# A two-layer spectral and MLP-mixer kernel: stores on GpSimd's queue, u split over two products, an earlier scale, and one weight load moved ahead

## The chip, the cores and the metric

The kernel runs on one core of a Trainium2 chip. The metric is the device time of one execution in microseconds (us), the median of several runs. Engines are called as in the profile: PE (TensorE), DVE (VectorE), ACT (ScalarE), POOL (GpSimd), SP (SyncE, which here only issues DMAs).

## The reference

Two kinds of layer alternate, twice, on x of 2048 tokens by 640 channels. The change lies in the second kind, B.

```python
def _A_ref(x, w_r, w_i):                       # spectral filter
    X = jnp.fft.rfft2(x, axes=(-2, -1)) * (w_r + 1j * w_i)
    return jnp.fft.irfft2(X, s=(S, D), axes=(-2, -1))

def _B_ref(x, w1, b1, w2, b2):                 # MLP over the tokens
    h = _layernorm(x, axis=-1)                 # (B, 2048, 640)
    u = jnp.einsum("bsd,sf->bdf", h, w1) + b1  # (B, 640, 1728)
    u = _gelu(u)                               # tanh form
    y = jnp.einsum("bdf,fs->bds", u, w2) + b2  # (B, 640, 2048)
    return y.transpose(0, 2, 1)

x = x + _A_ref(_layernorm(x), A_w_r, A_w_i)
x = x + _B_ref(_layernorm(x), B_w1, B_b1, B_w2, B_b2)
x = x + _A_ref(_layernorm(x), A_w_r, A_w_i)
x = x + _B_ref(_layernorm(x), B_w1, B_b1, B_w2, B_b2)
```

## The kernel before, in words

`run()` goes through the two layers. In each the spectral filter comes first and the MLP behind it; the MLP of layer 1 is `b1st`, that of the last layer `b2nd`. All large products run on PE in float16 with each operand split in two halves, high and low: a product is the sum high x high + low x high + high x low. The splits of weights cost ACT one pass (high half, `wh`) and DVE one (low half, `wl`), and so it is with the activations: DVE makes `uh` and `ul` from the gelu's output `uf` (`usplit`).

**`b1st`.** The first product runs over 14 tiles of w1 (`ft` counts them; `SEQ` gives the order in which tiles come: 6, 13, 0, 7, 1, 8, 2, 9, 3, 10, 4, 11, 5, 12, so that a pair of tiles with even and odd `ft` is d and d+7). Each of these is 96 matmuls, 16 steps `j` of 6. Raw weights in float32 are loaded by `wload` on SP's queue, in two parts into two buffers; ACT sums their squares (`scan1`, output `junk`), and a short chain of DVE and PE steps (`scale1`: a DVE reduction into `sqb`, PE's product with `ones`, a few DVE steps on one column) makes the scale by which the tile is split (`wsplit`). The steps of that chain are called by `step(m)` at places that are written into the loops by hand, tile m being one of w1 (m below 14) or of w2 (m = 14 and up).

Since the last layer uses the same w1 and w2, layer 1 stores what it has split: `wstore` stores w1's halves (`w1A..`, 36 stores of 256 KB) and some of w2's, and `wssplit` makes four sums of each pair of w1 tiles (S1 to S4, made by `wsum` in float32) into high and low halves, in one of two buffers `sp`, and stores them (`w1S..`, 24 stores of 512 KB). The last layer uses them for products by Strassen's scheme. All these stores stand on SP's queue, among the raw loads.

The gelu of a tile (ACT: `t`, square `q`, tanh; DVE: `q`, `uf`) follows its product. The scale of u is known from `scale_u`, called at ft = 11, j = 8. The 14 `usplit`s come in the last product (ft = 13, from j = 6 on, tiles 0 to 9) and behind the loop (10, 11, 13, 12). The second product then takes 16 tiles of w2, with all 14 tiles of u for each, in `SEQ`'s order.

**`b2nd`.** The same two products, by Strassen's scheme: `one` is a list of 42 products with w1 (N1 = 42), `two` one of 56 with w2, numbered n from 0. A product of the second list is 21 matmuls; the first four are 18 each at first, and the seventh tile of u (`LATE`) is added for all four at n = 3. The weights go through six buffers in turn (`place`: wo0, wo1, and wl, wh twice). `fetch` loads a stored part into the next buffer on SP's queue; `form`, `hi` and `lo` make a sum of raw parts (DVE `S`), its high half (ACT) and its low half (DVE) instead, from raw w2 loaded by `load2`. `xload` loads rows of x to which the result is added (`xt`). The first six parts of the second list, A11.0 to A22.1, are w2's and were stored by layer 1; these are the quarters spoken of here, A22.1 the sixth. In the loop before, turn n fetches part n + 4, after that turn's product is issued.

Each engine works through its instructions in order. The order on each engine is that of the code where `self.pin` is set, and elsewhere that of a scheduler, which sets instructions by their dependencies and costs; `b1st`'s two products lie outside the pin. Buffers are reused in turn, and a writer waits for the last reader.

Of the kernel before, what the change touches and what calls it, by code (L numbers as in the profile page):

```python
# [20 lines left out]
NJ, NG, NFT = 16, 16, 14  # L21
# [8 lines left out]
SEQ = [t + 7 * i for t in (6, 0, 1, 2, 3, 4, 5) for i in range(2)]  # L30
# [36 lines left out]
class Layers:  # L67
# [813 lines left out]
    def wstore(self, m, w):  # L881

        k, t, n = self.wtile(m)
        e = t % NQ if k else t % 7
        if (not 6 <= e < 8) if k else e == 6:
            return
        for c in (0, 1) if t == e else (1,):
            a, q = f"A{1 + (t > e)}{c + 1}", n // 2
            st = (self.ws2 if k else self.ws1)[e][a]
            for i in range(2):  # L890
                self.nc.sync.dma_start(st[:, i], w[i][:, c * q:c * q + q])

    def wsum(self, m, a):

# [6 lines left out]
    def wssplit(self, m, a):  # L901

        d = SEQ[m - 1]
        s = self.s1p[:, d:d + 1]
        w = self.t(self.pz, [128, 2, 8, 128], F16, "sp", 2)
        self.T.activation(w[:, 0], self.sums[a], AF.Identity, scale=s)
        self.V.scalar_tensor_tensor(w[:, 1], self.sums[a], s, w[:, 0], op0=ALU.mult, op1=ALU.subtract)
        self.nc.sync.dma_start(self.ws1[d][a], w)

    def b1st(self, li):  # L910
        nc, A = self.nc, self.A
# [13 lines left out]
        for j in range(NJ):  # L925
            self.h.append((self.hh[j], ph.tile([128, 2, 320], F16, name=f"hl{j}_{self.n}")))
            V.tensor_tensor(self.h[j][1], self.hf[j], self.hh[j], op=ALU.subtract)
            if j == 11:
                next(sc[2])
        self.pin = False  # L930
        self.pop("hf")
# [5 lines left out]
        uf = [pf.tile([128, 2, 320], F32, name=f"uf{f}_{self.n}") for f in range(NFT)]  # L937
# [23 lines left out]
        def usplit(ft, t):  # L961
            V.tensor_scalar(uh[ft], t, self.su, None, op0=ALU.mult)
            c = slice(0 if ft < NFT - 1 else 64, 128)
            V.scalar_tensor_tensor(ul[ft][c], t[c], self.su[c], uh[ft][c], op0=ALU.mult, op1=ALU.subtract)
            if ft == NFT - 1:
                V.tensor_copy(ul[ft][:64], uh[ft][:64])
                G.memset(uh[ft][64:], 0.0)
# [18 lines left out]
        w = self.w.pop(0), self.w.pop(1)  # L986
        pss = self.big(), self.big()
        self.both_high(pss, w, prod)
        for ft in range(NFT):
            if ft < 2:  # L990
                ps, run = pss[ft], rest(ft, pss[ft], w[ft])
                if ft:
                    self.wopen(2)
            else:
                ps = self.big()
                w2 = self.w.pop(ft)
                run = both(ft, ps, w2)
                ahead(ft, w2)
            steps = prep(ft)
            for j in run:  # L1000
                if ft % 2 and ft < NFT - 2 and 11 <= j < 15:
                    self.wsum(ft + 2, ("S1", "S3", "S2", "S4")[j - 11])
                if ft > 1:
                    m = ft + 1 - ft % 2
                    d = SEQ[m - 1]
                    if ft < m and j == 7:
                        q = [self.st[0][:, t:t + 1] for t in (d, d + 7)]
                        V.tensor_tensor(self.s1p[:, d:d + 1], *q, op=ALU.min)
                    if j in ((9, 14) if ft < m else (1, 7)):
                        self.wssplit(m, {9: "S1", 14: "S2", 1: "S3", 7: "S4"}[j])  # L1010
                if ft == 0:
                    if j in (6, 7):
                        step(2)
                elif ft == 1:
                    if j in (1, 2):
                        next(steps)
                    if j in (8, 10):
                        self.scan1(3, (j // 2 - 4,))
                    if j == 15:
                        step(3)  # L1020
                else:
                    if ft == 2 and j in (4, 5):
                        step(3)
                    if ft == 2 and j in (5, 6):
                        self.scan1(4, (j - 5,))
                    if ft == 2 and j == 7:
                        step(4)
                    if j in ((6, 8) if ft == 2 else (2, 4)):
                        next(steps)
                    if ft == 2 and j in (10, 11) or ft > 2 and j in (4, 5):  # L1030
                        step(ft + 2)
                    if j == 8 and ft == NFT - 3:
                        self.scale_u()
                    if j in (11, 13):
                        self.scan1(ft + 3, (j // 2 - 5,))
                    if j == 15:
                        step(ft + 3)
                    if ft == NFT - 1 and 6 <= j:
                        usplit(j - 6, uf[j - 6])
            dup, i = ft == 1, SEQ[ft]  # L1040
            pv, bb, c1 = ps[:, :, :320], self.b1[:, i:i + 1], self.ct[0][:, i:i + 1]
            if dup:

                sw = self.t(p, [128, 2, 320], F32, "sw", 1)
                T.activation(sw[:64], pv[64:], AF.Copy)
                T.activation(sw[64:], pv[:64], AF.Copy)
                V.tensor_tensor(sw, pv, sw, op=ALU.add)
                pv = sw
            t = self.t(p, [128, 2, 320], F32, "t", 2)
            q = self.t(p, [128, 2, 320], F32, "q", 2)  # L1050
            T.activation(t, pv, AF.Identity, scale=c1, bias=bb)
            T.activation(q, pv, AF.Square, scale=c1, bias=bb)
            V.scalar_tensor_tensor(q, q, 1.0 / GC, t, op0=ALU.add, op1=ALU.mult)
            T.activation(q, q, AF.Tanh, scale=GS * GC)
            V.scalar_tensor_tensor(uf[i], q, 1.0, t, op0=ALU.add, op1=ALU.mult)
        for k in (10, 11, 13, 12):
            usplit(k, uf[k])
        self.pop("uf")
        self.pop("b1")
# [25 lines left out]
        for j in range(NJ):  # L1085
# [14 lines left out]
            if tail:  # L1100

                order.sort(key=lambda q: q[1])
                st = self.t(p, [128, 2, 6], F32, "st", 2)
# [55 lines left out]
    def b2nd(self, li):  # L1159
# [29 lines left out]
        N1, NP = len(one), len(one) + len(two)  # L1189
# [17 lines left out]
        def fetch(n):  # L1207
            if n >= NP or not kept(n):
                return
            d, a, _ = ops[n]  # L1210
            w = place(n, 8 if n < N1 else 7)
            if n < N1:
                nc.sync.dma_start(w, self.ws1[d][a])
            else:
                nc.sync.dma_start(w, self.ws2[E[d]][a])
                if a[2] == "2":
                    G.memset(w[64:, :, 6], 0.0)
# [163 lines left out]
        for d in range(ND):  # L1381
            i = {a: at[d, a] for a in PB}
# [139 lines left out]
        def xload(d):  # L1522
            if d < NQ:
                xts[d] = self.t(p, [128, 2, 2, 320], F32, "xt", 3)
                for i in range(2):
                    nc.sync.dma_start(row(d, i), self.xs[li][E[d] + NQ * i])
# [59 lines left out]
        for (d, a), n in at2.items():  # L1586
            if a[0] == "S":
                n -= N1
                todo[n - 4 - (d > 1 and a == "S1")].append(lam(form, N1 + n, p))
        xload(0)  # L1590
        xload(1)
        for d in range(2):
# [4 lines left out]
        for n in range(NP2 + 1):  # L1597
            if n < NP2:
                d, a, _ = ops[N1 + n]
                if n > 3 or n % 2 == 0:  # L1600
                    big = self.big()
                bank[n] = big[:, n % 2 if n < 4 else 0, :320]
                product(n, rest if n < 4 else rest + [LATE], stop=n > 3)
            if n == 3:
                for k in range(4):
                    product(k, [LATE], start=False)
            if n in (2, 4):
                xbias(n // 2 - 1)
            for k in {0: (), 1: (), 2: (), 3: (), 4: (0, 1, 2, 3)}.get(n, (n - 1,)):
                evict(k)  # L1610
                q = ops[N1 + k][0]
                left[q] -= 1
                if not left[q] and q + 3 < NQ:
                    xload(q + 3)
                    extra[n + 4].append(lam(xbias, q + 3))
            if n == 5:
                xbias(2)
            if n > 2:
                hi(N1 + n + 3)
            if n > 3:  # L1620
                lo(N1 + n + 2)
            for e in todo[n]:
                e()
            fetch(N1 + n + 4)
            for e in extra[n]:
                e()
            if n in (6, 10) or n < NP2 and d > 1 and a == "A12":
                d = n // 4 + 1 if n < 14 else d + 2
                for b in ("A21", "A22", "A11", "A12") if d < NQ else ():
                    load2(d, b)  # L1630
# [293 lines left out]
```

## Time and profile before

| | |
|---|---|
| runs | 1026.18, 1022.86, 1020.11 us; median 1022.86 |
| profiled execution | 1021.25 us, span 1019.0, mean granted clock of PE 0.976 |
| DMA | 176.44 MB, mean 173 GB/s |
| queues | hardware 68024 packets, 168.94 MB; software (POOL's) 1440 packets, 6.17 MB |

PE is the busiest engine. The first product of layer 1 lies at about 192 to 367 us of the span, its second follows; the last layer's MLP begins near 713 with the loads of the stored parts, and its second product near 851. The windows of the profile give busy us for each engine in a stretch, then PE's granted clock as a fraction of full speed, the busy share of the DMA engines and GB/s. In timeline rows stand start, length, engine, line, operation, out<-in with shapes and a count; in brackets how long the engine was idle before the row and what it waited for. A record's length holds some pipelining: matmuls of 0.30 us start every 0.136 us at full clock. Most rows bear L59, the line of the helper that records them; tiles tell them apart.

### The profile page before, as it was taken

How to read it: one execution, taken by the hardware profiler on the slowest of the kernel's cores; microseconds unless marked ns; L12 is line 12 of the kernel's file. 1: busy time of each engine (PE TensorE's matmuls, PEld its weight loads, DVE VectorE, ACT ScalarE, POOL GpSimd, SP SyncE). 2: the span in 40 equal slices, each digit the busy share in tenths (PEclk: the TensorE clock that was granted, in tenths of full speed). 3: DMA queues.
4: the chain of work that ended last, by engine and by line, in shares of the span. 5: the costliest groups of instructions: out<-in, count | busy, mean ns of one | idle time of the engine just before them, and what ended most of it. 6: DMA issues, size and time to landing. Idle time of an engine off the chain costs nothing.

```text
span 1019.0 us, 20974 instructions
## 1 busy us (share of the span) xinstructions
PE 969.9 (95%) x8235; PEld 722.0 (71%) x8235; DVE 782.7 (77%) x1493; ACT 576.7 (57%) x890; POOL 266.1 (26%) x442
## 2 busy tenths in 40 slices
PE   3879999999999989999999899999999999999998
PEld 2768777667777767777777688776777776677775
DVE  7968978998777884666666689789956546988885
ACT  5847668697666655555553377685644435444531
POOL 6927857500000001222222288574000000000000
PEclk9599999999999999999999799999999999999999
DMA  7855356657666547464433455464544547555411
GB/s 232 279 176 169 115 164 223 215 183 282 218 224 198 196 149 240 137 196 126 125 103 103 143 171 172 128 223 144 175 160 163 165 161 295 172 167 193 144 44 52
DMA packets 69562, 176.44 MB, mean 173 GB/s; under 512 B 7996, under 2 KB 15320, under 8 KB 69464
## 3 DMA queue, kind: packets, MB, share of 16 engines
q1 hardware_dynamic: 68024, 168.94, 50.4%
q0 software_dynamic: 1440, 6.17, 2.0%
q8 instruction: 64, 1.05, 0.4%
q14 instruction: 34, 0.28, 0.1%
HBM read 127.24 MB, written 47.84 MB: 172 GB/s over the span
## 4 chain that ended last, share of the span: by engine, by line
PE 41%; DVE 26%; DMA 11%; ACT 10%; issue 6%; POOL 5%; SPq 0%; ACTq 0%; DVEq 0%; POOLq 0%
PE ps L59 41%; DVE wl L59 5%; DMA raw<-w 4%; DMA xt<-x 3%; DVE f L59 3%; DVE st L59 3%; POOL eo L59 2%; DVE s1l L59 2%; ACT wh L59 2%; DMA w1S<-sp 2%; DVE Yl L59 2%; DVE xt L59 2%; POOL xt L59 1%; ACT z L59 1%; ACT junk L59 1%
## 5 line engine op out<-in xcount | busy, mean ns | idle before, releaser
L59 PEld LDWEIGHTS <-wh 128*128 128x128 f16 x2602 | 252.7, 98 | 103.3 <-DMA wh<-w2A 2.7
L59 PEld LDWEIGHTS <-wl 128*128 128x128 f16 x1610 | 157.7, 98 | 63.9 <-issue 2.5
L59 PE MATMUL ps<-ul,wh 128*128 128x320 f16 x448 | 133.9, 301 | 1.4 <-DVE ul L59 1.4
L59 PE MATMUL ps<-uh,wl 128*128 128x320 f16 x448 | 134.0, 301 | 0.0
L59 PE MATMUL ps<-uh,wh 128*128 128x320 f16 x416 | 124.9, 300 | 1.3 <-DVE s L59 1.3
L59 PE MATMUL ps<-hl,wh 128*128 128x320 f16 x496 | 102.0, 299 | 0.2 <-DVE hl L59 0.2
L59 PEld LDWEIGHTS <-wo 128*128 128x128 f16 x756 | 74.0, 98 | 28.7
L59 ACT ACTIVATE junk<-raw 128x896 bf16<-128x896 f32 (+1 forms) x60 | 59.5, 992 | 42.9 <-DMA raw<-w 42.7
L59 DVE SCALAR_TENSOR_TENSOR wl<-raw,s,wh 128x896 f16<-128x896 f32 (+2 forms) x64 | 74.2, 1161 | 12.3 <-ACT wh L59 12.1
L59 POOL TENSOR_TENSOR r<-v,mh 128x1 f32<-128x1 f32 x64 | 36.4, 569 | 143.5 <-DVE nm L59 134.1
L59 PE MATMUL ps<-tDi,Yh 128*128 128x322 f16 x320 | 71.3, 300 | 0.2
L59 DVE TENSOR_TENSOR f<-eo 128x256 f32<-128x256 f32 (+1 forms) x124 | 39.1, 368 | 38.6 <-POOL eo L59 38.0
L59 ACT ACTIVATE wh<-raw,s 128x896 f16<-128x896 f32 (+2 forms) x68 | 67.4, 1010 | 1.6 <-DVE s L59 1.6
L59 POOL TENSOR_TENSOR xt<-xt,ec 128x320 f32<-128x320 f32 x64 | 52.4, 841 | 33.1 <-DVE xt L59 32.9
L59 ACT ACTIVATE z<-xt,nb,r 128x640 f32<-128x640 f32 x31 | 28.5, 919 | 56.9 <-POOL z L59 44.5
L59 PE MATMUL ps<-ph,tS 128*128 128x321 f16 (+2 forms) x288 | 58.6, 286 | 1.3 <-DVE tb L59 1.3
L59 DVE BATCH_NORM_STATS2 st<-xt 128x6 f32<-128x320 f32 x126 | 55.3, 481 | 5.5 <-DMA xt<-x 4.4
L59 PE MATMUL ps<-u,wo 128*128 128x320 f16 x420 | 58.8, 299 | 0.0
L59 PE MATMUL ps<-hha,wh 128*128 128x320 f16 x288 | 58.1, 299 | 0.0
L59 POOL TENSOR_TENSOR eo<-z 128x320 f32<-128x320 f32 x62 | 53.3, 881 | 17.0 <-ACT z L59 15.1
L59 PE MATMUL ps<-tM,f 128*128 128x128 f32 x160 | 36.4, 392 | 21.8 <-DMA xt<-x 11.4
L59 PE MATMUL ps<-tDi,Yl 128*128 128x322 f16 x192 | 55.7, 299 | 1.5 <-DVE Yl L59 1.5
(247 smaller groups left out, 2348.4 us busy)
## 6 DMA issues: line engine op xcount, KB each, us to landing
xt<-x SPq DMA_DIRECT2D x79, 320.0 KB
raw<-w SPq DMA_DIRECT2D x32, 512.0 KB
w<-w SPq DMA_DIRECT2D x48, 321.0 KB
x<-xt SPq DMA_DIRECT2D x47, 320.0 KB
raw<-w SPq DMA_DIRECT2D x32, 448.0 KB
raw<-w2z SPq DMA_DIRECT2D x32, 448.0 KB
w1S<-sp SPq DMA_DIRECT2D x24, 512.0 KB
out<-xt SPq DMA_DIRECT2D x15, 320.0 KB
```

The source lines that it names most:

```text
L59: i = f(*a, **k)
```

## The change

Four edits. The stores of w1's parts and of the sums go on POOL's queue instead of SP's. DVE's reduction for tile 2's scale comes two steps sooner in the loop that makes the low halves of h, and PE's side of it two steps later. The 14 splits of u are spread: eight over the product ft = 12, four over ft = 13, two behind. In the last layer the fetches of the fifth and sixth quarter stand ahead of the first loads of x and raw w2.

```diff
--- before.py
+++ after.py
@@ -888,7 +888,7 @@
             a, q = f"A{1 + (t > e)}{c + 1}", n // 2
             st = (self.ws2 if k else self.ws1)[e][a]
             for i in range(2):
-                self.nc.sync.dma_start(st[:, i], w[i][:, c * q:c * q + q])
+                (self.nc.sync if k else self.nc.gpsimd).dma_start(st[:, i], w[i][:, c * q:c * q + q])
 
     def wsum(self, m, a):
 
@@ -905,7 +905,7 @@
         w = self.t(self.pz, [128, 2, 8, 128], F16, "sp", 2)
         self.T.activation(w[:, 0], self.sums[a], AF.Identity, scale=s)
         self.V.scalar_tensor_tensor(w[:, 1], self.sums[a], s, w[:, 0], op0=ALU.mult, op1=ALU.subtract)
-        self.nc.sync.dma_start(self.ws1[d][a], w)
+        self.nc.gpsimd.dma_start(self.ws1[d][a], w)
 
     def b1st(self, li):
         nc, A = self.nc, self.A
@@ -925,7 +925,7 @@
         for j in range(NJ):
             self.h.append((self.hh[j], ph.tile([128, 2, 320], F16, name=f"hl{j}_{self.n}")))
             V.tensor_tensor(self.h[j][1], self.hf[j], self.hh[j], op=ALU.subtract)
-            if j == 11:
+            if j == 9:
                 next(sc[2])
         self.pin = False
         self.pop("hf")
@@ -1009,7 +1009,7 @@
                     if j in ((9, 14) if ft < m else (1, 7)):
                         self.wssplit(m, {9: "S1", 14: "S2", 1: "S3", 7: "S4"}[j])
                 if ft == 0:
-                    if j in (6, 7):
+                    if j in (8, 9):
                         step(2)
                 elif ft == 1:
                     if j in (1, 2):
@@ -1035,8 +1035,9 @@
                         self.scan1(ft + 3, (j // 2 - 5,))
                     if j == 15:
                         step(ft + 3)
-                    if ft == NFT - 1 and 6 <= j:
-                        usplit(j - 6, uf[j - 6])
+                    if ft == NFT - 2 and j % 2 or ft == NFT - 1 and j % 3 == 0 and 0 < j < 13:
+                        i = SEQ[j // 2 if ft == NFT - 2 else 7 + j // 3]
+                        usplit(i, uf[i])
             dup, i = ft == 1, SEQ[ft]
             pv, bb, c1 = ps[:, :, :320], self.b1[:, i:i + 1], self.ct[0][:, i:i + 1]
             if dup:
@@ -1053,7 +1054,7 @@
             V.scalar_tensor_tensor(q, q, 1.0 / GC, t, op0=ALU.add, op1=ALU.mult)
             T.activation(q, q, AF.Tanh, scale=GS * GC)
             V.scalar_tensor_tensor(uf[i], q, 1.0, t, op0=ALU.add, op1=ALU.mult)
-        for k in (10, 11, 13, 12):
+        for k in SEQ[12:]:
             usplit(k, uf[k])
         self.pop("uf")
         self.pop("b1")
@@ -1587,6 +1588,8 @@
             if a[0] == "S":
                 n -= N1
                 todo[n - 4 - (d > 1 and a == "S1")].append(lam(form, N1 + n, p))
+        fetch(N1 + 4)
+        fetch(N1 + 5)
         xload(0)
         xload(1)
         for d in range(2):
@@ -1621,7 +1624,8 @@
                 lo(N1 + n + 2)
             for e in todo[n]:
                 e()
-            fetch(N1 + n + 4)
+            if n > 1:
+                fetch(N1 + n + 4)
             for e in extra[n]:
                 e()
             if n in (6, 10) or n < NP2 and d > 1 and a == "A12":
```

On DVE, at the end of `b1st`'s first product, where `uh`, `ul` are u's halves, `sp` the low halves of the sums S1 to S4 of the last pair, and `wl_744` the low half of w2's first tile, before:

```order
L59 TENSOR_SCALAR uh1_546_3331<-uf1_547_3362,su_130 128x640
L59 SCALAR_TENSOR_TENSOR sp_733_5133<-S1_717_5003,sp1_79,sp_733_5133 128x1024
L59 SCALAR_TENSOR_TENSOR sp_735_5170<-S2_720_5021,sp1_79,sp_735_5170 128x1024
...
L59 SCALAR_TENSOR_TENSOR sp_745_5211<-S3_719_5013,sp1_79,sp_745_5211 128x1024
L59 SCALAR_TENSOR_TENSOR sp_748_5266<-S4_721_5030,sp1_79,sp_748_5266 128x1024
...
L59 SCALAR_TENSOR_TENSOR ul10_546_3354<-uf10_547_3371,su_130,uh10_546_3340 128x640
L59 SCALAR_TENSOR_TENSOR ul11_546_3355<-uf11_547_3372,su_130,uh11_546_3341 128x640
L59 SCALAR_TENSOR_TENSOR wl_744_5204<-raw_708_4898,s1_73,wh_743_5203 128x896
L59 SCALAR_TENSOR_TENSOR q_739_5190<-q_739_5190,t_738_5189 128x640
L59 SCALAR_TENSOR_TENSOR wl_744_5204<-raw_709_4900,s1_73,wh_743_5203 128x896
L59 SCALAR_TENSOR_TENSOR uf5_547_3366<-q_739_5190,t_738_5189 128x640
```

and after:

```order
L59 SCALAR_TENSOR_TENSOR ul0_546_3344<-uf0_547_3361,su_130,uh0_546_3330 128x640
L59 SCALAR_TENSOR_TENSOR ul7_546_3351<-uf7_547_3368,su_130,uh7_546_3337 128x640
L59 SCALAR_TENSOR_TENSOR sp_733_5143<-S1_717_5003,sp1_79,sp_733_5143 128x1024
...
L59 SCALAR_TENSOR_TENSOR sp_735_5186<-S2_720_5021,sp1_79,sp_735_5186 128x1024
...
L59 SCALAR_TENSOR_TENSOR sp_745_5229<-S3_719_5013,sp1_79,sp_745_5229 128x1024
...
L59 SCALAR_TENSOR_TENSOR ul10_546_3354<-uf10_547_3371,su_130,uh10_546_3340 128x640
L59 SCALAR_TENSOR_TENSOR sp_748_5286<-S4_721_5030,sp1_79,sp_748_5286 128x1024
L59 TENSOR_SCALAR uh4_546_3334<-uf4_547_3365,su_130 128x640
L59 SCALAR_TENSOR_TENSOR wl_744_5222<-raw_708_4898,s1_73,wh_743_5221 128x896
L59 SCALAR_TENSOR_TENSOR ul4_546_3348<-uf4_547_3365,su_130,uh4_546_3334 128x640
...
L59 SCALAR_TENSOR_TENSOR wl_744_5222<-raw_709_4900,s1_73,wh_743_5221 128x896
L59 SCALAR_TENSOR_TENSOR uf5_547_3366<-q_739_5208,t_738_5207 128x640
```

S1 and S2 stood next to each other, and S3 and S4 near them; now tiles of u come first, and the four sums are spread over the stretch, S4 just ahead of `wl_744`. Eleven tiles of u stand wholly or partly ahead of `wl_744` in both.

On POOL, which held in this stretch only the `MEMSET` of `uh13` before, the end of the row of stores after (w1A.. are w1's halves, w1S.. the sums; the number behind is the pair):

```order
L891 DMA w1A12_5_118<-wl_711_4905 128x1024
L59 MEMSET uh13_546_3343 64x640
L908 DMA w1S1_5_120<-sp_733_5143 128x2048
L891 DMA w1A22_5_119<-wh_729_5063 128x1024
L891 DMA w1A22_5_119<-wl_730_5064 128x1024
L908 DMA w1S2_5_121<-sp_735_5186 128x2048
L908 DMA w1S3_5_122<-sp_745_5229 128x2048
L908 DMA w1S4_5_123<-sp_748_5286 128x2048
```

The stores stand in the order of the code, each behind the wait of the one ahead of it.

On SP in the last layer, around the two fetches `w2A22_6` and `w2A22_7` (the fifth and sixth quarter), with `xt` the rows of x and `raw` those of w2, before:

```order
L1215 DMA wl_1548_11898<-w2A12_7_128 128x1792
L1215 DMA wh_1562_11965<-w2A22_6_126 128x1792
L1526 DMA xt_1550_11921<-x3_6_172 128x640
...
L1526 DMA xt_1551_11924<-x3_15_181 128x640
L1397 DMA raw_1552_11927<-w2z 128x896
...
L1397 DMA raw_1559_11941<-w2z 128x896
L1526 DMA xt_1560_11943<-x3_0_166 128x640
L1526 DMA xt_1560_11943<-x3_8_174 128x640
L1215 DMA wh_1563_11986<-w2A22_7_129 128x1792
L1397 DMA raw_1579_12141<-w2z 128x896
```

and after:

```order
L1216 DMA wl_1548_11898<-w2A12_7_128 128x1792
L1216 DMA wh_1550_11921<-w2A22_6_126 128x1792
L1216 DMA wh_1551_11924<-w2A22_7_129 128x1792
L1527 DMA xt_1552_11927<-x3_6_172 128x640
...
L1527 DMA xt_1553_11930<-x3_15_181 128x640
L1398 DMA raw_1554_11933<-w2z 128x896
...
L1398 DMA raw_1561_11947<-w2z 128x896
L1527 DMA xt_1562_11949<-x3_0_166 128x640
L1527 DMA xt_1562_11949<-x3_8_174 128x640
L1398 DMA raw_1579_12141<-w2z 128x896
```

The fifth quarter stood ahead of x and raw already; the sixth moves ahead of six loads of x and eight of raw w2.

## Prediction

> **What bounds the kernel now.** First the busy time of the engines, then windows around the stages that the change touches, then PE's waits in the timeline there.
>
> ```profile
> PE 969.9 (95%) x8235; PEld 722.0 (71%) x8235; DVE 782.7 (77%) x1493; ACT 576.7 (57%) x890; POOL 266.1 (26%) x442
> ```
> ```profile
> 240.00:280.00 40.00, 40.00 (x299) 28.82 (x298) 30.93 (x50) 26.97 (x37) 0.00 (x0) 1.00 0.67 236
> 340.46:368.20 27.74, 27.74 (x208) 20.00 (x206) 26.41 (x44) 16.31 (x22) 0.00 (x0) 1.00 0.49 159
> 380.40:383.80 3.40, 3.40 (x15) 1.94 (x14) 0.87 (x2) 2.72 (x4) 0.00 (x0) 0.51 0.95 321
> 868.20:872.00 3.80, 3.80 (x18) 2.14 (x16) 3.80 (x5) 1.59 (x2) 0.00 (x0) 0.55 0.24 51
> ```
>
> PE is busy 95% of the span. In the windows (length; then busy us of PE, PEld, DVE, ACT, POOL; granted clock; DMA share; GB/s) it has no gap at all from 240 to 280 and from 340 to 368: while layer 1 stores its weight parts, nothing that frees SP's queue can help a PE that never waits. The change can gain only where PE does wait near its edits: in the first product's opening, at the turn from first to second product, and in the last layer; the rows follow with each part. Two of these places are followed by a stretch at about half clock (0.51 and 0.55), so a wait there costs more than itself. Measured against no change, about 0.5% (5.1 us) can be told apart here.
>
> **The third scale sooner: nothing.** Timeline rows of ACT, DVE and PE:
>
> ```profile
> 199.11 0.19 ACT L59 ACTIVATION_READ_ACCUMULATOR junk<-raw 128x1 f32 x1
> 201.74 0.15 DVE L59 TENSOR_REDUCE sqb<-sq 128x1 bf16<-128x2 f32 x1
> 201.81 3.02 DVE L59 TENSOR_TENSOR hl<-hf,hh 128x640 f16<-128x640 f32 x4
> 201.95 0.18 PE L59 MATMUL ps<-sqb,ones 128*128 128x1 bf16 x1 [1.08 <-DVE sqb L59]
> 204.88 0.57 PE L59 MATMUL ps<-hl,wh 128*128 128x320 f16 x3 [0.15 <-DVE hl L59]
> ```
>
> PE waits 1.08 us for the sum of squares. Two low halves earlier (3.02/4 us each) the reduction would run at about 200.3, after ACT's scan ended at 199.3, so DVE does not stall. But PE's later wait is for the last low half, which ends at 204.8 in either order, since DVE does the same work. PE only waits later. I take 0; the bounds are 0 and the whole 1.23.
>
> **Stores on POOL's queue, and u split over two products: 0.8 us.** PE at the turn from the first to the second product, and the chain behind it:
>
> ```profile
> 372.00 0.30 PE L59 MATMUL ps<-ul,wh 128*128 128x320 f16 x1 [0.73 <-DVE ul L59]
> 379.04 0.30 PE L59 MATMUL ps<-uh,wh 128*128 128x320 f16 x1 [1.30 <-DVE s L59]
> 379.95 0.30 PE L59 MATMUL ps<-ul,wh 128*128 128x320 f16 x1 [0.62 <-DVE ul L59]
> ```
> ```profile
> 366.43 11.58 SPq L851 DMA_DIRECT2D raw<-w  x4
> ```
> ```profile
> 367.06 1.15 DVE L59 SCALAR_TENSOR_TENSOR wl<-raw,s,wh 128x896 f16<-128x896 f32 x1
> 371.94 0.95 ACT L59 ACTIVATE junk<-raw 128x896 bf16<-128x896 f32 x1 [1.12 <-DMA raw<-w]
> 378.43 0.55 DVE L59 TENSOR_SCALAR uh<-uf,su 128x640 f16<-128x640 f32 x1
> 379.02 0.88 DVE L59 SCALAR_TENSOR_TENSOR ul<-uf,su,uh 128x640 f16<-128x640 f32 x1
> ```
>
> PE waits 0.73, then 1.30 and 0.62 for the last tile's halves, 2.65 in all, and then runs 15 matmuls at 0.51 clock where 3.40 us would hold 25 (one per 0.136 us): 1.4 more. The splits that move are not what the last tile waits for. Its chain is: DVE's low half of w2's first quarter ends at 368.2 (call it X), which frees a raw buffer; SP loads it, ACT scans it, ACT makes t and q of the last tile behind the scan, and DVE's last low half is done at 379.9, X plus 11.7. The other wait (0.73) goes, but is absorbed: PE then reaches the last tile 0.73 sooner. So the turn moves only as X moves.
>
> In both orders eleven u tiles are split before X, so DVE's work up to X is the same. It was busy 26.41 of 27.74 us there: X can come at most 1.3 sooner. What decides whether it does are the stores. After the change the sums S2 to S4 of the last pair are split late, one by one, and use two buffers: S3's high half on ACT waits until S1's store has landed, S4's until S2's has, and ACT's in-order queue holds the gelu of the next tile and w2's high halves behind each.
>
> ```profile
> 222.92 5.16 DMA w1S<-sp
> 290.42 2.63 DMA w1S<-sp
> ```
> ```profile
> L59 POOL DMA_DIRECT2D tIM<-tIM x6: 576/625/629, 131.3 to 668.1; - x6
> DMA to landing us min/median/max: 4.3/5.2/8.1
> ```
> ```profile
>   ACT sp L59: 7.0, 5
> ```
>
> A 512 KB store from SP's queue took 2.6 to 5.2 us. The nearest row for POOL's queue is its 512 KB loads: issue 0.6 us, landed after 4.3 to 8.1, median 5.2. Sixty issues of 0.6 us cost nothing on POOL itself: the windows above show it at 0.00. Going down the new order with the durations of these rows, X is about 366.7 while a store lands within 4.4 us; beyond, each further us costs two, since two such waits stand in series. At 5.2 that gives 368.3, no gain; at 4.3 the full 1.5. Stores here are as large as these loads but the DMA engines are half idle (share 0.49), so I take the middle, 0.8. The half clock stays, since about 2 us of idling remain. Bounds: a loss of 5.9 at 8.1 us, a gain of 2.65 + 1.4 = 4.05 if the waits vanish.
>
> The Trainium skill ("DMA: Bandwidth & Descriptors", Anatomy of one DMA) fits a DMA issued by GpSimd as 2.0 us plus its bytes at 436 GB/s; that is an estimate of 3.2 us for 512 KB, and by it the turn would gain all of 1.5. The loads of this trace took longer, 4.3 at least.
>
> The rounds before that must stand it too: five times ACT waits for these buffers already, 7.0 us in all. PE needs 2 x 96 x 0.136 = 26.1 us for a pair of products; DVE, busy 30.93 of 40, has 5.9 us free in it. Two waits longer by up to 2.9 each fit, so up to about 7 us of landing PE stays fed.
>
> **The sixth quarter sooner in the last layer: 3.3 us.**
>
> ```profile
> 847.81 0.32 SPq L1215 DMA_DIRECT2D wh<-w2A  x1
> 848.18 1.85 SPq L1526 DMA_DIRECT2D xt<-x  x4
> 850.07 6.02 SPq L1397 DMA_DIRECT2D raw<-w2z  x8
> 856.89 1.94 SPq L1526 DMA_DIRECT2D xt<-x  x2
> 859.61 0.32 SPq L1215 DMA_DIRECT2D wh<-w2A  x1
> ```
> ```profile
> 850.88 5.05 PE L59 MATMUL ps<-u,wo 128*128 128x320 f16 x36
> 862.28 3.02 PE L59 MATMUL ps<-u,wh 128*128 128x320 f16 x21
> 867.68 4.70 PE L59 MATMUL ps<-u,wh 128*128 128x320 f16 x21 [2.38 <-DMA wh<-w2A]
> 872.22 5.87 PE L59 MATMUL ps<-u,wo 128*128 128x320 f16 x42
> 877.92 5.87 PE L59 MATMUL ps<-u,wl 128*128 128x320 f16 x42
> ```
> ```profile
> 851.03 8.52 DMA raw<-w2z
> ```
> ```profile
> 861.18 1.08 DVE L59 TENSOR_TENSOR S<-raw,raw 128x896 f32<-128x896 f32 x1
> 865.27 0.55 DVE L59 SCALAR_TENSOR_TENSOR xt<-ps,c,xt 128x320 f32<-128x320 f32 x1 [1.88 <-ACT m L59]
> 867.80 1.14 DVE L59 SCALAR_TENSOR_TENSOR wo<-S,sp,wo 128x896 f16<-128x896 f32 x1
> 882.51 1.14 DVE L59 SCALAR_TENSOR_TENSOR wh<-S,sp,wh 128x896 f16<-128x896 f32 x1
> ```
>
> SP issues the load that PE waits 2.38 us for at 859.61, behind 14 others. Moved ahead of them, it waits only until its buffer's last product ends, 850.9 when the next one starts, and lands well ahead of 865. A product is 21 matmuls: 5.70/2 = 2.85 us. Without the wait the sixth quarter starts at 862.28 + 2.85 = 865.13 and the next product at 867.98 instead of 872.22: 4.24 us, 2.38 of waiting and 1.86 of half clock. Next late is DVE: its low half for that product ends at 868.94 where PE would want it at 868.25 (its third matmul), and that of the sixth product from there at 883.65, or 883.4 without a wait of its own, against 883.2: 0.69 + 0.2 are given back, since DVE runs almost without a gap from 866 to 889. That leaves 3.35. What the load is moved past is the xt and raw loads: they slip by some 3 us, the time that SP stands at the buffer (848.2 to 850.9). By the chain of waits a raw landed at 859.55, and DVE first adds raws at 861.18: 1.6 us to spare, and behind it DVE has a gap of 1.88 us; together they cover the slip, so I cost it at nothing. Were that cover missing, each low half comes up to 3 us later and the gain falls to 0.4; were DVE's halves sooner, it is 4.24.
>
> **The sum.** 0 + 0.8 + 3.35 = 4.15 us off the profiled execution's 1021.25 (span 1019.0 and 2.25 around it): 1017.1. The median of the runs is 1.6 above that execution; I give half of this back: 1017.9.
>
> **The rivals.** Forecast (0.40): as summed, 3 to 6 us gained.
>
> Given back (0.20): the quarter is there, but raws slip and DVE's low halves become PE's wait, and X stays; 0.4 to 2.5 us gained, 1019 to 1021. For it: SP stands 3 us and DVE has no gap. Here belongs a rule of the Trainium skill ("SBUF — State Buffer", SBUF: two separate sides): GpSimd cannot write the descriptors of its DMAs while DVE runs an operation in a mode that takes both ports, so stores on that queue can starve. Were a store held for one uh split (0.55 us) at each of the two waits in series, X would move by 1.1 and the turn lose 0.3 instead. The POOL issues above, 576 to 629 ns, show no such hold.
>
> All comes through (0.24): the waits at the turn vanish so that the clock does not fall, 4.05, with 4.24 at the last layer and some of the front's 1.23: 8.3 to 9.5, 1012 to 1013. For it: both low-clock stretches follow idling of about 2 us, and the rounds of the first layer have slack. Against: X can move only 1.3.
>
> Slower (0.16): stores from POOL land late. From about 6.8 us the turn loses more (2 x 1.65) than the last layer brings; at 8.1, the longest load, X is 5.9 later, and in each of five rounds two waits longer by 3.7 exceed the 5.9 free by 1.5: 5.9 to 13.4 lost less 3.35 gained, 1024 to 1031. For it: POOL's stores stand in one queue, each behind the next's wait. Against: the DMA engines are a third to a half idle there.
>
> **How the numbers follow.** Faster by over 0.5%: all of the third case and the upper part of the first, 0.40. Slower: 0.15 of the last. The rest, 0.45, lies within. The range leaves out the far ends of the third and last case: 1010.5 to 1026.
>
> **What would show it.** In the changed profile: no wait of PE for wh<-w2A near 865, clock 1.0 from 868 to 872, instead a wait for DVE below 1 us. At the turn the two waits for the last tile in place, after a low half of w2 that ends at 366.5 to 368.5. ACT's wait for sp not much over 7 us, stores landing in 3 to 5.5. PE's wait for sqb gone, the one for hl longer by as much. Wrong would be any wait of PE for wl or wh between 218 and 368, or one at 860 to 875 for xt or raw.

## The result, and the profile after

The changed kernel takes 1020.1 us (median of 20 runs), the one before 1023.4 in the same runs: a ratio of 0.9971 (95% interval 0.9959 to 0.9983), 3.0 us faster (1.7 to 4.2). Its profiled execution took 1019.09 us, span 1017.3, 1.7 below the span before.

The windows of the changed kernel over the stretches that the prediction showed, and over one new one (360.5 to 364.5):

```profile
340.46:368.20 27.74, 25.42 (x178) 17.61 (x177) 27.43 (x57) 17.47 (x23) 7.49 (x12) 0.94 0.53 174
360.50:364.50 4.00, 3.98 (x20) 2.44 (x21) 4.00 (x8) 2.03 (x3) 1.98 (x2) 0.62 0.47 189
380.40:383.80 3.40, 3.27 (x25) 2.23 (x24) 2.06 (x7) 1.39 (x3) 0.00 (x0) 1.00 0.86 262
868.20:872.00 3.80, 3.09 (x24) 2.00 (x23) 3.21 (x6) 2.60 (x4) 0.00 (x0) 1.00 0.95 383
```

Both stretches at half clock are gone (380 and 868 stand at 1.00), but the end of layer 1's first product, where PE had no gap before, is now 2.3 us short of busy, with a slow stretch of its own.

**The opening.** PE's timeline, before:

```profile
197.99 1.25 PE L59 MATMUL ps<-hh,wh 128*128 128x320 f16 x8
209.36 0.43 PE L59 MATMUL ps<-hha,wh 128*128 128x320 f16 x2
```

and after:

```profile
198.64 1.25 PE L59 MATMUL ps<-hh,wh 128*128 128x320 f16 x8
204.05 0.43 PE L59 MATMUL ps<-hl,wh 128*128 128x320 f16 x2 [0.30 <-DVE hl L59]
204.78 0.57 PE L59 MATMUL ps<-hl,wh 128*128 128x320 f16 x3 [0.30 <-DVE hl L59]
205.52 4.64 PE L59 MATMUL ps<-hl,wh 128*128 128x320 f16 x33 [0.17 <-DVE hl L59]
210.00 0.43 PE L59 MATMUL ps<-hha,wh 128*128 128x320 f16 x2
```

PE comes 0.65 us later to this place in this execution, through work that the change does not touch, and leaves it 0.64 later. The wait for the sum of squares is gone and three waits for low halves of h stand in its place.

**The turn.** PE's timeline of the changed kernel shows one large wait where there were three; then the chain to the end of layer 1: DVE's second low half of w2's first tile (X in the prediction; from here on X is the time at which it starts), SP's loads of raw weights and of x, ACT's and DVE's first use of x, and PE's wait at the end of the layer:

```profile
360.52 0.16 PE L59 MATMUL ps<-sqb,ones 128*128 128x1 bf16 x1 [2.32 <-DVE sqb L59]
385.90 0.17 PE L59 MATMUL ps<-sqb,ones 128*128 128x1 bf16 x1
```
```profile
369.70 1.14 DVE L59 SCALAR_TENSOR_TENSOR wl<-raw,s,wh 128x896 f16<-128x896 f32 x1
377.42 2.88 SPq L851 DMA_DIRECT2D raw<-w  x2
384.62 3.21 SPq L1076 DMA_DIRECT2D xt<-x  x3
393.59 2.42 ACT L59 ACTIVATE xt<-xt,b2s 128x640 f32<-128x640 f32 x3 [7.23 <-DMA xt<-x]
394.45 0.88 DVE L59 SCALAR_TENSOR_TENSOR xt<-ps,c,xt 128x640 f32<-128x640 f32 x1 [5.71 <-ACT xt L59]
566.00 0.28 PE L59 MATMUL ps<-tM,fh 128*128 128x128 f16 x2 [2.00 <-ACT fh L59]
```

The same places before:

```profile
385.29 0.17 PE L59 MATMUL ps<-sqb,ones 128*128 128x1 bf16 x1
377.69 0.33 SPq L851 DMA_DIRECT2D raw<-w  x1
382.23 3.06 SPq L1075 DMA_DIRECT2D xt<-x  x3
390.67 2.44 ACT L59 ACTIVATE xt<-xt,b2s 128x640 f32<-128x640 f32 x3 [6.68 <-DMA xt<-x]
391.53 0.88 DVE L59 SCALAR_TENSOR_TENSOR xt<-ps,c,xt 128x640 f32<-128x640 f32 x1 [4.84 <-ACT xt L59]
563.18 0.29 PE L59 MATMUL ps<-tM,fh 128*128 128x128 f16 x2 [1.05 <-ACT fh L59]
```

PE itself is as late behind the turn (0.61 us at the product with `ones` near 385) as it was ahead of it: what the new wait and its slow stretch cost, the old ones had cost. But the layer ends 2.82 us later. That follows the other chain: X is 2.64 later, the first result is added to x 2.92 later, and the end is 2.82 later. Between X and x stand raw loads, whose buffers DVE's low halves set free (the last one that x stands behind is issued when the low half that starts at 376.51 before, at 378.79 after, is done), and the constants of the next layer, some 4 us of SP's queue.

From its third tile on the chain keeps a pace of its own. DVE adds a tile to x about every 12.14 us in both kernels (411.03, 423.17, 435.32 before; 413.94, 426.09, 438.22 after). PE's products with `ones` come every 12.00 in the kernel before (444.46, 456.46, 468.46); in the changed one they come every 12.00 up to 445.07 and every 12.13 or 12.14 from 457.11 on (469.25, 481.38). So PE gains on the chain until it has caught up, and then goes at the chain's pace.

**The last layer.** SP and PE of the changed kernel:

```profile
850.11 3.58 SPq L1216 DMA_DIRECT2D wh<-w2A  x2
```
```profile
853.18 5.05 PE L59 MATMUL ps<-u,wo 128*128 128x320 f16 x36
864.59 5.87 PE L59 MATMUL ps<-u,wh 128*128 128x320 f16 x42
871.44 5.61 PE L59 MATMUL ps<-u,wo 128*128 128x320 f16 x40 [0.71 <-DVE wo L59]
876.88 5.87 PE L59 MATMUL ps<-u,wl 128*128 128x320 f16 x42
```

The wait for the sixth quarter is gone (42 matmuls in one piece). PE enters this product 2.30 us later than before (853.18 against 850.88), and starts the row of `wl` 1.04 sooner (876.88 against 877.92): 3.34 us gained, with 0.71 of waiting for DVE's low half kept.

### The profile page after: what moved, and what is told of

The parts are those of the page before. It is cut to its first block, busy times and chain, and to the rows that moved or that the text cites. A ratio compares the mean times of both kernels' runs of the same rounds, so it can differ in the third digit from the quotient of the medians.

```text
span 1017.3 us, 20999 instructions
## 1 busy us (share of the span) xinstructions
PE 968.7 (95%) x8235; PEld 719.4 (71%) x8235; DVE 782.9 (77%) x1493; ACT 577.6 (57%) x890; POOL 299.9 (29%) x502
## 3 DMA queue, kind: packets, MB, share of 16 engines
q8 instruction: 64, 1.05, 0.4%
## 4 chain that ended last, share of the span: by engine, by line
PE 41%; DVE 27%; issue 10%; ACT 9%; POOL 7%; DMA 6%; SPq 0%; POOLq 0%; ACTq 0%; DVEq 0%
PE ps L59 41%; DVE wl L59 5%; DVE f L59 3%; DVE st L59 3%; POOL eo L59 3%; DMA xt<-x 2%; DVE s1l L59 2%; ACT wh L59 2%; DVE xt L59 2%; DVE Yl L59 2%; DMA w1S<-sp 1%; POOL xt L59 1%; ACT z L59 1%; DMA raw<-w 1%; DVE hl L59 1%
```

## The experiments

Each was run against the kernel before on the same chip in five rounds. Differences in us are the ratio less one, times the median of before, measured beside it.

| kernel | ratio (95% interval) | us |
|---|---|---|
| all four edits (the change) | 0.9971 (0.9959 to 0.9983) | -3.0 |
| e1 last layer alone | 0.9970 (0.9955 to 0.9985) | -3.1 |
| e2 stores alone | 1.0016 (1.0002 to 1.0029) | +1.6 |
| e3 u split alone | 0.9983 (0.9970 to 0.9995) | -1.7 |
| e4 change, stores on SP | 0.9953 (0.9939 to 0.9967) | -4.8 |
| e5 change, sums' stores on SP | 0.9988 (0.9976 to 1.0000) | -1.2 |
| e6 change, three sum buffers | 0.9937 (0.9923 to 0.9951) | -6.4 |
| e7 as e4, x loads first | 0.9942 (0.9926 to 0.9959) | -5.9 |
| e8 change, x loads first | 0.9930 (0.9917 to 0.9943) | -7.2 |
| e9 as e8, three buffers | 0.9922 (0.9904 to 0.9940) | -8.0 |
| e10 as e4, three buffers | 0.9917 (0.9896 to 0.9939) | -8.5 |
| e11 change, early reduction | 0.9965 (0.9949 to 0.9980) | -3.6 |
| e12 as e7, three buffers | 0.9912 (0.9896 to 0.9928) | -9.0 |

### One edit at a time

e1, on the kernel before:

```diff
+        fetch(N1 + 4)
+        fetch(N1 + 5)
         xload(0)
...
-            fetch(N1 + n + 4)
+            if n > 1:
+                fetch(N1 + n + 4)
```

> The kernel before with only the fourth edit (fifth and sixth quarter fetched ahead of x and raw w2). Theory A (the edits of layer 1 cost about 2 us together, which the last layer's edit outweighs): 3.3 to 4 us faster than before, more than all four edits together, with PE waiting 0.7 us for a low half near 868 and no half clock there. Rival B (the fourth edit's gain is partly given back behind it, and layer 1 adds some): 1 to 2.5 us faster, less than all four together.

It gave 3.1 us (1.5 to 4.6), between the two theories' ranges and as much as the whole change. The layer-1 edits together are worth about nothing; theory A's 2 us lost there is not seen in the medians, nor is a gain.

e2, on the kernel before:

```diff
-                self.nc.sync.dma_start(st[:, i], w[i][:, c * q:c * q + q])
+                (self.nc.sync if k else self.nc.gpsimd).dma_start(st[:, i], w[i][:, c * q:c * q + q])
...
-        self.nc.sync.dma_start(self.ws1[d][a], w)
+        self.nc.gpsimd.dma_start(self.ws1[d][a], w)
```

> The kernel before with only the first edit (stores on POOL's queue), DVE's order as before. Theory A1 (a store issued by POOL holds its sum's buffer longer, so ACT and DVE run later in each round, the low half of w2's first tile ends 2 us later, and with it the loads of x and the end of layer 1): 1 to 3 us slower than before. Rival A2 (the order of the u splits is what makes it late): within 0.7 us of before.

It is 1.6 us slower (0.2 to 3.0), as theory A1 had it; the lower end of the interval still lies within A2's 0.7. In its profile the end of layer 1 is 1.56 later than before (564.74 against 563.18). The expectation takes DVE's order to be as before; the trace has another one, which is shown below with e10. The view of the tile w1S shows how long a store took from POOL's queue, and ACT's waits for the buffers of the sums, which were 7.0 us in all before:

```profile
  ACT sp L59: 12.7, 6
DMA to landing us min/median/max: 2.9/3.2/6.8
```

e3, on the kernel before:

```diff
-                    if ft == NFT - 1 and 6 <= j:
-                        usplit(j - 6, uf[j - 6])
+                    if ft == NFT - 2 and j % 2 or ft == NFT - 1 and j % 3 == 0 and 0 < j < 13:
+                        i = SEQ[j // 2 if ft == NFT - 2 else 7 + j // 3]
+                        usplit(i, uf[i])
...
-        for k in (10, 11, 13, 12):
+        for k in SEQ[12:]:
```

> The kernel before with only the third edit (u split over two products), stores on SP. Theory A1: within 0.7 us of before, the wait for the last tile's halves smaller, and a wait of PE for tile 14's sum of squares in its place, since DVE's reduction stands behind the second sum in the new order whatever queue stores. Rival A2: 1.5 to 3 us slower, the low half of w2's first tile ending 2 us later than before.

It is 1.7 us faster (0.5 to 3.1): better than both theories had it, and A2 falls. Its timeline has PE's new wait for a sum of squares, with the stores on SP, as A1 said:

```profile
358.65 0.16 PE L59 MATMUL ps<-sqb,ones 128*128 128x1 bf16 x1 [1.65 <-DVE sqb L59]
```

e4 is the changed kernel without e2's two lines.

> The changed kernel with its stores back on SP's queue (edits two, three and four alone). Theory A1: 1.5 to 2.5 us faster than the changed kernel, 5 us faster than before. Rival A2: as the changed kernel, 3 us faster than before.

At 4.8 us faster than before (3.4 to 6.2) it beats the change by 1.8, and it is the sum of e1 and e3 (3.1 + 1.7). So the four edits add up: -3.1 + 1.6 - 1.7 = -3.2, measured -3.0; the second edit is left for nothing, as the rows of the opening show. By these medians the loss lies in the stores, though the intervals of e4 and of the change overlap.

### Why the stores cost

e5 is the change with only the sums' stores back on SP's queue (the last line of e2's diff undone).

> The changed kernel with the stores of the sums back on SP's queue; only the 36 stores of w1's halves stay on POOL's. Theory C1 (the stores cost because a sum's buffer, one of two, is held longer: from the end of DVE's low half over POOL's issue to the landing): 1.2 to 2.2 us faster than the changed kernel, 4.2 to 5.2 faster than before. Rival C2 (any store on POOL's queue costs, by its in-order queue or by traffic): no more than 0.7 us from the changed kernel, 2.3 to 3.7 faster than before.

A miss for both: 1.2 us faster than before (0 to 2.5), some 1.8 slower than the change. The stores of the halves cost on POOL's queue by themselves, 3.6 against e4, and ACT's waits for the sums' buffers (9.8 us) are then hardly above e4's (9.4). C1 does not explain that. In e5's profile PE waits 0.53 and 1.58 us for low halves of w1, at 303.74 and 331.62, where e4 has no wait: 2.1 of the 3.6 are lost there, ahead of the turn.

e6:

```diff
-        w = self.t(self.pz, [128, 2, 8, 128], F16, "sp", 2)
+        w = self.t(self.pz, [128, 2, 8, 128], F16, "sp", 3)
```

> The changed kernel with three buffers for the sums instead of two, all stores on POOL's queue. Theory C1: ACT's waits for these buffers, 11.1 us in the changed kernel, fall below 4, and it is 1.2 to 2.2 us faster than the changed kernel, 4.2 to 5.2 faster than before. Rival C2: the waits fall, the time stays within 0.7 us of the changed kernel.

It is 3.4 us faster than the change, at 6.4 faster than before (5.0 to 7.9). ACT's waits for these buffers fall to half, not below 4:

```profile
  ACT sp L59: 5.3, 5
```

That looked like C1, until the same was done on SP's queue.

> Edits two, three and four with the stores on SP's queue and three buffers for the sums. Theory C1 (what POOL's queue cost was the longer hold of two buffers, and with three the queue does not matter): within 0.7 us of the kernel with three buffers and POOL's queue, 5.7 to 7.1 us faster than before. Rival G (with enough buffers POOL's queue is the better one, since SP's loads no longer stand behind the stores' waits): 4.0 to 5.5 us faster than before.

e10 is e4 with e6's line: 8.5 us faster than before (6.2 to 10.6), 3.7 faster than e4 and better than both theories had it. So by the medians a third buffer is worth about the same on either queue, and POOL's queue is not cheaper for it (e6 is 2.0 behind e10, with intervals that overlap). What does show in all five pairs of kernels whose code differs by the stores' queue alone is X. Counted from the start of PE's product with `ones` near 344 to the start of the second low half of w2's first tile, with SP's queue and with POOL's:

| | SP | POOL |
|---|---|---|
| before (and e1); e2 | 23.1 (23.7) | 25.5 |
| e4; the change | 23.3 | 24.7 |
| e7; e8 | 24.4 | 24.8 |
| e10; e6 | 19.5 | 23.3 |
| e12; e9 | 19.0 | 23.2 |

These stand in single profiles, and two whose code is the same up to there lie as much as 1.1 apart (e4 and e7). X is later with POOL in every pair, by 0.4 to 4.2 us. Why it is stays open, and one rival was not tested: the queue is not all that changes. The scheduler sets the order of ACT and DVE in this stretch, and with the stores on POOL's queue it sets another one, in round after round. ACT at the third sum of the first round, before:

```profile
226.76 1.15 ACT L59 ACTIVATE wh<-raw,s 128x1024 f16<-128x1024 f32 x1
228.95 1.15 ACT L59 ACTIVATE sp<-S,sp 128x1024 f16<-128x1024 f32 x1 [0.41 <-DMA w1S<-sp]
```

and in the changed kernel:

```profile
230.31 1.15 ACT L59 ACTIVATE sp<-S,sp 128x1024 f16<-128x1024 f32 x1 [2.82 <-DMA w1S<-sp]
231.99 2.17 ACT L59 ACTIVATE wh<-raw,s 128x1024 f16<-128x1024 f32 x2
```

Before, ACT does a high half of w1 and a step of the gelu while the first store is under way; in the changed kernel these stand behind the wait. e4 has the first order and a wait of 0.64, e2 the second and one of 3.25. So with two buffers the lateness begins in this first round, and the runs do not separate the queue from the order that came with it. It could also be the order in one queue, where each store waits behind the one before, or the traffic of loads that are issued sooner.

### What sets the end of layer 1

e7 is e4 with one block moved:

```diff
         self.a0_open()
-        for q in range(4):
-            self.a0_load_m(q)
-        self.a0_load()
...
         xts = [load(0), load(1)]
+        for q in range(4):
+            self.a0_load_m(q)
+        self.a0_load()
```

> The kernel with edits two, three and four and the stores on SP, and in addition layer 1 issues its first two loads of x ahead of the loads of the next layer's constants. Theory D (the end of layer 1 follows the low half of w2's first tile by 196 us, by way of the loads of x behind it on SP's queue, in all six kernels so far): PE's last wait of the layer falls from 2.0 to about 1.0 us, its 12.14 us rhythm from 500 on returns to 12.00, and it is 1 to 2 us faster than without this, 5.8 to 6.8 faster than before. Rival E (PE's own waits at the turn set the end of the layer): within 0.5 us of the kernel without it, 4.3 to 5.3 faster than before.

It is 5.9 us faster than before (4.2 to 7.5), 1.1 more than e4; the intervals overlap. DVE adds the first result at 385.97 instead of 391.99, and the wait for `fh` at the end of the layer is gone; only the one for `fl` behind it is left, 0.94 sooner than in e4 (567.18):

```profile
385.97 0.88 DVE L59 SCALAR_TENSOR_TENSOR xt<-ps,c,xt 128x640 f32<-128x640 f32 x1 [2.36 <-ACT xt L59]
566.24 0.29 PE L59 MATMUL ps<-tM,fl 128*128 128x128 f16 x1 [4.48 <-DVE fl L59]
```

> The changed kernel, stores on POOL, with the same two loads of x ahead of the constants. Theory D: 1.5 to 2.5 us faster than the changed kernel, 4.5 to 5.5 faster than before, since what the stores made late no longer sets the end of the layer. Rival E: within 0.5 us of the changed kernel, 2.5 to 3.5 faster than before.

e8 is the change with the same block moved: 7.2 us faster than before (5.8 to 8.5), 4.2 faster than the change, clear of noise and twice what theory D said. Rival E falls. Its wait for `fl` at the end of the layer comes at 566.25, where e7 has it at 566.24: with x ahead the layer ends at the same time in both profiles, whatever the stores' queue, and the change had more to gain up to there (its own wait for `fl` comes at 569.62). Without the block moved, PE's wait at the end of the layer lies between 195.6 and 196.3 us behind X in nine of the ten profiles (197.1 in e1's). Behind DVE's first addition to x it lies 171.55 to 171.65 us in all ten. The plainest is e10, where PE was 2.7 us later than before at the mark near 344 (346.67 against 344.00) and had no wait at the turn at all:

```profile
346.67 0.17 PE L59 MATMUL ps<-sqb,ones 128*128 128x1 bf16 x1
```
```profile
366.13 1.14 DVE L59 SCALAR_TENSOR_TENSOR wl<-raw,s,wh 128x896 f16<-128x896 f32 x1
562.13 0.29 PE L59 MATMUL ps<-tM,fh 128*128 128x128 f16 x2 [2.00 <-ACT fh L59]
```

PE 2.7 later, X 0.9 sooner than before, the end of the layer 1.05 sooner: it goes with X.

e11 takes the new wait of 2.32 us away:

```diff
-                    if j == 15:
+                    if j == (13 if ft == NFT - 2 else 15):
                         step(ft + 3)
```

> The changed kernel with DVE's reduction for w2's first tile called two steps sooner in the product ft = 12, which puts it ahead of the low half of sum S2 and of the second low half of w1's last tile. PE's wait of 2.3 us for it, and the half clock behind it, go. Theory D (the end of layer 1 follows the low half of w2's first tile, not PE): within 0.8 us of the changed kernel, 2.3 to 3.8 us faster than before, PE waiting for the last tile of u instead. Rival E (PE's waits at the turn count in full): 2 to 4 us faster than the changed kernel, 5 to 7 faster than before.

It is 3.6 us faster than before (2.0 to 5.2), within 0.6 of the change: theory D. The wait is gone, X stays nearly where it was (0.36 later), PE waits at five other places of the turn instead, 3.9 us in all, and the layer ends at 565.79 against 566.00:

```profile
370.06 1.14 DVE L59 SCALAR_TENSOR_TENSOR wl<-raw,s,wh 128x896 f16<-128x896 f32 x1
372.73 0.16 PE L59 MATMUL ps<-sqb,ones 128*128 128x1 bf16 x1 [1.73 <-DVE sqb L59]
565.79 0.28 PE L59 MATMUL ps<-tM,fh 128*128 128x128 f16 x2 [2.00 <-ACT fh L59]
```

### The versions put together

> The changed kernel with three buffers for the sums and with the first two loads of x ahead of the constants. Theory D (both act on one chain, from the low half of w2's first tile over the loads of x to the end of layer 1, so that the second adds only what the first leaves until PE itself is the bound): 6.9 to 8.5 us faster than before. Rival F (two separate costs, 3.4 and 4.2 us over the changed kernel): 9.5 to 11.5 us faster than before.

e9 is the change with e6's line and e7's block: 8.0 us faster than before (6.1 to 9.8). The two bring 3.4 and 4.2 over the change by themselves, 5.0 together: one chain, as theory D had it, though the interval just reaches rival F's 9.5.

> Edits two, three and four, stores on SP's queue, three buffers for the sums, and the first two loads of x ahead of the constants. By theory D what three buffers bring and what the x loads bring act on one chain and PE is the next bound: 8 to 10 us faster than before, so the fastest of all, or equal to the one with three buffers on SP's queue. Rival G (POOL's queue better): within 0.7 us of the same kernel with POOL's queue, 7.3 to 8.7 us faster than before.

e12 is e7 with e6's line: 9.0 us faster than before (7.4 to 10.6), a median of 1013.63, the fastest of all, and clearly faster than the change. With e10 and e9 it lies inside the noise, so that theory D holds, and whether rival G does is not decided.

## Why the prediction was right, and where not

**The whole.** 4.15 us were forecast, 3.0 (1.7 to 4.2) measured; the time, 1017.9 forecast, came out at 1020.1, inside the range, with the kernel before at 1023.4 beside it where the forecast had started from 1022.86. That is the lower edge of the likeliest case (3 to 6 us); the interval also reaches into the case "given back" (0.4 to 2.5 us, 1019 to 1021). The larger term was right in its mechanism. That the smaller one did no more harm is luck: its two parts, neither of them forecast, cancel.

**The opening** was right to its mechanism: the wait is handed on to the last low half of h, and PE leaves 0.64 later where it came 0.65 later.

**The last layer** was right in each step: 4.24 available, 0.69 kept by DVE's low half (0.71 measured, and no second wait of 0.2), 3.35 forecast, 3.34 in the profile and 3.1 in e1's runs. SP did stand at the buffer (3.58 us for the two fetches), and the slip of x and raw loads was covered.

**The turn** is the term that failed: 0.8 gained was forecast, the runs give -1.7 for the split and +1.6 for the stores, so about nothing; in the profiled execution the layer ends 2.2 later (2.82 less 0.65). Three steps of it were wrong. First, X was placed by counting DVE's work from 340.46, as if DVE came there at the same time; it came 3.9 us later, to the first uh split before and after:

```profile
340.46 0.55 DVE L59 TENSOR_SCALAR uh<-uf,su 128x640 f16<-128x640 f32 x1
```
```profile
344.40 0.54 DVE L59 TENSOR_SCALAR uh<-uf,su 128x640 f16<-128x640 f32 x1
```

From there to X DVE took 25.30 us instead of 26.60: the 1.3 that the prediction held possible came, and the loss lay ahead. The rounds ahead already ran late, with ACT waiting 11.1 us in all for the sums' buffers instead of 7.0. The argument that these fit into DVE's free 5.9 us a round held for PE, not for DVE's own lateness. Second, the price of a store was taken from loads of the same size, 4.3 to 8.1 us; it was 3.2 in the median:

```profile
  ACT sp L59: 11.1, 6
DMA to landing us min/median/max: 2.9/3.2/6.4
```

The Trainium skill's fit ("DMA: Bandwidth & Descriptors", Anatomy of one DMA), 3.2 us by that estimate, is this median. The first two stores took 6.4 and 5.1, and ACT's wait of 2.82 us shown above is for the first of them. By the prediction's rule a landing of 3.2 should have brought X 1.5 sooner, and it came later: the rule priced the last four sums and left out the first round. Third, and most: the prediction said that the turn moves as X moves, by PE's wait for the last tile of u. The first half stands, and e10 and e11 show it; but the path runs over SP, where the loads of x stand behind raw loads that wait for DVE's low halves from X on, and behind constants, and from there over the additions to x, tile by tile, to the end of the layer. PE's waits at the turn, on which that part was spent, moved from place to place at no cost that the runs show.

**What was not seen**: PE's wait for a sum of squares, that of w2's second tile (the expectations count it as tile 14 or as the first; by the code it is 15). DVE's reduction for it, before:

```profile
344.33 0.15 DVE L59 TENSOR_REDUCE sqb<-sq 128x1 bf16<-128x2 f32 x1
```

and after:

```profile
360.24 0.14 DVE L59 TENSOR_REDUCE sqb<-sq 128x1 bf16<-128x2 f32 x1
```

It stands behind S2's low half in both orders; S2's moved away from S1's, down behind seven splits and w1's last low halves, and took it along, past the time at which PE's product with `ones` comes (358). The prediction followed the u splits through the new order, and not what stood between them. It had named a wait of PE between 218 and 368 for weights as a sign that it is wrong; a wait of 0.17 for wl came, at 329.

**The rivals.** The one that lost by late stores had the right place, the rounds of the sums, and its reason holds for the first two stores only (6.4 and 5.1 us; the median of all 24 is 3.2). The rule of the Trainium skill that stood with the case "given back" shows, small: POOL's clearing of `uh13`, 0.63 us before, took 1.72 where DVE ran two uh splits beside it, and the issue of two stores next to such splits 0.75 and 1.44 instead of 0.54:

```profile
347.29 1.72 POOL L59 MEMSET uh<- 64x640 f16 x1 [4.04 <-DVE ul L59]
351.53 0.75 POOL L908 DMA_DIRECT2D w1S<-sp  x1 [2.52 <-DVE sp L59]
362.62 1.44 POOL L908 DMA_DIRECT2D w1S<-sp  x1 [1.53 <-ACT junk L59]
```
```profile
347.44 1.00 DVE L59 TENSOR_SCALAR uh<-uf,su 128x640 f16<-128x640 f32 x2
351.16 1.00 DVE L59 TENSOR_SCALAR uh<-uf,su 128x640 f16<-128x640 f32 x2
362.94 1.00 DVE L59 TENSOR_SCALAR uh<-uf,su 128x640 f16<-128x640 f32 x2
```

The trace agrees with the Trainium skill ("SBUF — State Buffer", SBUF: two separate sides) in that POOL is held while DVE runs these. The hold is no cause for the loss: the store of 0.75, that of S1, is the one that ACT waits for and lost 0.2 us, no later sum uses the buffer of the one of 1.44, and in e2, where the stores cost 1.6 us too, no store of a sum took over 0.54 to issue.

## What to carry to other kernels

A wait of the busiest engine is worth something only if the path behind it to the next common point runs through that engine: here PE's waits at the turn could be moved and made larger or smaller at no cost that the runs show, because a chain of loads, additions and normalisations, started by one DVE instruction, reached the end of the layer later than PE did. Look for it by the distance between an early instruction and the end of the stage in several kernels: a constant (196 us here) names the chain. And where a scheduler sets the order, look at what a DMA's move to another queue does to the order of the other engines before you price it by the moved instructions alone; here that cost was not settled, and the fastest version left the stores where they were, added a buffer and set two loads ahead of less urgent ones.

## What was not expected of the hardware

A wait of PE of about 2.4 us was not always followed by half clock. In three profiles of the last layer with the wait for the sixth quarter in them, 21 matmuls behind it took 4.70 us in two (waits of 2.38 and 2.44) and 3.02 in the third, behind a wait of 2.49:

```profile
868.73 3.02 PE L59 MATMUL ps<-u,wh 128*128 128x320 f16 x21 [2.49 <-DMA wh<-w2A]
```

At the turn it is the same: behind the changed kernel's wait of 2.32 the granted clock was 0.62 (360.5 to 364.5), behind e8's of 2.42 at the same place 1.00. The prediction's 1.86 us for that clock is therefore not a fixed price of the wait. The Trainium skill ("TensorE: Matmul & The Clock Gate", What's actually happening) has the clock fall after an idle window of about 3.4 us, in windows that run freely; here it fell after waits of 2.38 and 2.44, shorter than that. That it falls in one run and not in another fits windows that run freely; no run here tests it.
